# First stage of a fused forward-and-backward block re-ordered: gate row and grad_out loaded first, sines and norms of x in pinned orders, first w2^T products between the turns of grad_out

## The chip, the cores and the metric

The kernel runs on one core of a Trainium2 chip. A core has five engines, each with an instruction queue of its own that is worked in order: TensorE (PE in the profile; its weight loads are listed as PEld), VectorE (DVE), ScalarE (ACT), GpSimd (POOL) and SyncE (SP), which here only issues transfers. Engines wait for each other and for transfers through semaphores. Transfers run on 16 DMA engines that all queues share. The metric is the time of one execution on the device in microseconds (us).

## The reference

The reference computes one block and all its gradients. For x of 2048 tokens by 1024, with `c` a 1024-long condition:

```python
mod = (silu(c) @ w_mod)                      # six rows of 1024: sa, ca, ga, sb, cb, gb
h = layernorm(x) * (1 + ca) + sa
x = x + ga * irfft2(rfft2(h) * (w_r + 1j * w_i))
h = layernorm(x) * (1 + cb) + sb
x = x + gb * (gelu(layernorm(h) @ w1 + b1) @ w2 + b2)      # w1: 1024 x 3584
```

It returns x and, for a given `grad_out`, the gradients by x, w_r, w_i, w1, b1, w2, b2, c and w_mod. The Fourier transforms are computed in the kernel as matrix products with tables of sines and cosines, after the even and odd parts of h were split by additions and subtractions ("folds").

## The kernel before, in words

The program is written against a tile library. When the kernel is built, a planner gives every instruction a place in its engine's queue, and it chooses the engine where the code says `nc.any`. `tc.high_priority()` moves an instruction ahead in that plan, and `with tc.issue_after(ins)` pins what is written under it behind `ins`. Tiles that carry the same `tag` share memory, so a later tile waits for the last use of the earlier one.

The part that matters here is the first stage, up to the first spectral product (`pu`, line 472). It has four strands.

- **Rows of mod.** `mod_load` brings a 1024 x 512 block of w_mod (1 MB), `mod_block` (line 246) multiplies it with silu(c) in eight products into PSUM (`pm`, line 253), and DVE or ACT copies the result to a row (line 256). Row 5 is gb, row 1 is ca, row 0 is sa. The blocks use a ring of three buffers.
- **grad_out, turned.** `load_go` brings grad_out in four quarters of 1 MB. PE turns each in eight groups of four 128 x 128 transposes (`pt`, line 344), and DVE and ACT in turn copy a group out of PSUM, multiplied with gb per row (`gBoT`, lines 347 and 351). gb has to stand as a column for that (`gb_col`, line 339, from the little products `pc`, line 337). Four PSUM buffers of tag "f" serve these groups, and the same four serve the w2^T products below.
- **Sines.** `trig` (line 389) lets POOL make an integer index (line 373, into a ring of two index buffers), DVE mask it (line 396), and ACT take the sine (line 397). `gen_mats` does this for eight pieces of the row tables (smA, smB) and four of the column tables (em1), stores them to DRAM, and scales a copy of em1 on POOL (line 412).
- **x.** `load_tok` brings a chunk of 512 tokens, half of it by one SP transfer and half by two gathers that POOL issues (line 131). `ln_dve` or `ln_mix` computes mean and variance (BN statistics on DVE, lines 437 and 447; sums on ACT, lines 451 and 454), `ln_fin` the reciprocal root, `norm_act` (line 461) normalises on ACT in four instructions, and DVE multiplies with 1 + ca and folds (line 173). The first `pu` product needs all four chunks.

The time between is filled with the w2^T products: `ph_part` (line 678; `pp`, line 684) multiplies w2^T, loaded by a transposing transfer of 256 rows (`load_w2t`, line 301, two buffers), with gBoT. 28 row chunks of four quarters with eight products each are made in all; they are independent of x. ACT and DVE copy the results (lines 691, 694) and POOL issues their store (line 696). Further row blocks of mod are computed between them.

SP's queue before has this order: c, ca block 0, x0, ca block 1, gb block 0, grad_out 0, gb block 1, w2^T 0, grad_out 1, x1, grad_out 2 and 3, x2, x3, w2^T 1, then sa and the later blocks. POOL's has x's eight gathers ahead of all index work.

Of the kernel before, what the change touches and what calls it, by code (L numbers as in the profile page):

```python
# [11 lines left out]
BF16 = mybir.dt.bfloat16  # L12
# [23 lines left out]
def kernel(  # L36
# [88 lines left out]

    def load_tok(t4, src, i, eng=None):
# [3 lines left out]
        for q in range(2):  # L130
            nc.gpsimd.indirect_dma_start(out=t4[:, 1 + q, :], out_offset=None, in_=s3,
                                         in_offset=bass.IndirectOffsetOnAxis(ap=xidx[:, 2 * i + q:2 * i + q + 1], axis=0))
# [114 lines left out]
    def mod_block(r, h, wblk=None):  # L247
# [4 lines left out]
        for jc in range(NDC):  # L252
            nc.tensor.matmul(pm[:], lhsT=u_b[:, jc, :], rhs=wblk[:, jc, :], start=(jc == 0), stop=(jc == NDC - 1))
        dst = MOD_DST[r][:, h * KH:(h + 1) * KH]
        with tc.high_priority():
            nc.any.tensor_copy(out=dst, in_=pm[:])
        if r in (1, 4):
            nc.vector.tensor_scalar(out=dst, in0=dst, scalar1=1.0, scalar2=None, op0=ALU.add)

# [40 lines left out]
    def load_w2t(fg):  # L300
# [4 lines left out]
    gos = [reg.tile([P, 4, D], BF16, name="go0", tag="px1")[:], reg.tile([P, 4, D], BF16, name="go1", tag="smb")[:],  # L305
           fbuf[:, 2], fbuf[:, 3]]
# [28 lines left out]
    pc = ps_d("pc")  # L335
    for cch in range(NDC):
        nc.tensor.matmul(pc[:, cch:cch + 1], lhsT=gb_row[0:1, cch * P:(cch + 1) * P], rhs=ones_bf[0:1, 0:1], start=True, stop=True)
    with tc.high_priority():
        nc.vector.tensor_copy(out=gb_col[:], in_=pc[:, 0:NDC])
    for j in range(4):  # L340
        for cch in range(NDC):
            pt = psum.tile([P, BW], BF16, tag="f", name="pt", bufs=4)
            for a in range(4):
                nc.tensor.transpose(pt[:, a * P:(a + 1) * P], gos[j][:, a, cch * P:(cch + 1) * P], ident[:])
            if cch % 2 == 0:
                with tc.high_priority():
                    nc.vector.tensor_scalar(out=gBoT[j][:, cch, :], in0=pt[:], scalar1=gb_col[:, cch:cch + 1], scalar2=0.0,
                                            op0=ALU.mult, op1=ALU.add, accum_out=gu[:, j, cch:cch + 1])
            else:
                with tc.high_priority():  # L350
                    nc.scalar.activation(out=gBoT[j][:, cch, :], in_=pt[:], func=ACT.Identity, scale=gb_col[:, cch:cch + 1],
                                         accum_out=gu[:, j, cch:cch + 1])

# [17 lines left out]
    def pts(out, in0, s1, s2, o0, o1=None):  # L371
        kw = {} if o1 is None else {"op1": o1}
        nc.gpsimd.tensor_scalar(out=out, in0=in0, scalar1=s1, scalar2=s2, op0=o0, **kw)
# [15 lines left out]
    def trig(dst, colv, rowv, nrow, width, modn, cosine):  # L389
# [3 lines left out]
        for r in range(nrow):  # L393
            pts(idx[:, r * width:(r + 1) * width], colv, rowv[:, r:r + 1], sh, ALU.mult, ALU.add)
        n = nrow * width
        nc.vector.tensor_scalar(out=idx[:, 0:n], in0=idx[:, 0:n], scalar1=modn - 1, scalar2=None, op0=ALU.bitwise_and)
        nc.scalar.activation(out=dst, in_=idx[:, 0:n].rearrange("p (r w) -> p r w", w=width), func=ACT.Sin,
# [969 lines left out]
```

## Time and profile before

| | |
|---|---|
| median of 3 runs | 1463.76 us (1459.1 to 1466.73) |
| profiled execution | 1459.13 us; span of its trace 1457.3 us |
| PE busy | 1396.5 us, 96% of the span |
| DVE, ACT, POOL busy | 73%, 52%, 25% |
| gb's column copied (`gb_col`) | at 29.65 us |
| last scaled copy of grad_out | from 45.23, read out by 45.98 us |
| last fold of x (fourth chunk) | from 127.58 us |
| first spectral stage `pu` in full | 129.41 us |
| first product of the second layer (`pz`) | 343.87 us |

Times within the trace count from the start of the span. In a timeline row stand the start, the busy time, the engine and line, the operation with the tiles it writes and reads, the shape, the number of instructions merged into the row, and in brackets how long the engine had stood idle and what released it. The view by windows gives, for stretches of time, the busy time of each engine with the number of instructions, the clock that TensorE was granted (1.00 is full), the mean busy share of the DMA engines and GB/s.

### The profile page before, as it was taken

How to read it: one execution, taken by the hardware profiler on the slowest of the kernel's cores; microseconds unless marked ns; L12 is line 12 of the kernel's file. 1: busy time of each engine (PE TensorE's matmuls, PEld its weight loads, DVE VectorE, ACT ScalarE, POOL GpSimd, SP SyncE). 2: the span in 40 equal slices, each digit the busy share in tenths (PEclk: the TensorE clock that was granted, in tenths of full speed). 3: DMA queues.
4: the chain of work that ended last, by engine and by line, in shares of the span. 5: the costliest groups of instructions: out<-in, count | busy, mean ns of one | idle time of the engine just before them, and what ended most of it. 6: DMA issues, size and time to landing. Idle time of an engine off the chain costs nothing. (4 is left out here: it accounts for less than half of the span.)

```text
span 1457.3 us, 18411 instructions
## 1 busy us (share of the span) xinstructions
PE 1396.5 (96%) x6835; PEld 649.0 (45%) x6835; DVE 1058.4 (73%) x1483; ACT 752.2 (52%) x1065; POOL 366.1 (25%) x441
## 2 busy tenths in 40 slices
PE   5889999999999999999999999999999999999997
PEld 2434545444444444444444444344444445444443
DVE  5884786898799787887520889898467678898650
ACT  4675555857887766665305574342622434344211
POOL 6520451211112122122211011021245441222432
PEclk8999999999999999999999999999999999999999
DMA  9962473899887877697998275297699987766991
GB/s 333 286 214 70 142 235 115 270 255 337 257 203 278 259 250 233 201 264 241 277 297 245 74 271 185 107 270 176 181 217 254 254 233 213 194 191 180 297 279 65
DMA packets 358367, 324.28 MB, mean 223 GB/s; under 512 B 209386, under 2 KB 301056, under 8 KB 358022
## 3 DMA queue, kind: packets, MB, share of 16 engines
q1 hardware_dynamic: 324166, 207.71, 52.7%
q0 software_dynamic: 34112, 115.41, 22.6%
q8 instruction: 53, 0.87, 0.2%
q14 instruction: 36, 0.29, 0.1%
HBM read 162.06 MB, written 111.20 MB: 188 GB/s over the span
## 5 line engine op out<-in xcount | busy, mean ns | idle before, releaser
L684 PE MATMUL pp<-gBoT,wt 128*128 128x512 bf16 x896 | 197.9, 380 | 4.5 <-DMA wt<-in_B_w_dram 2.6
L950 PE MATMUL pg<-w1T,gzr 128*128 128x512 bf16 x896 | 197.1, 381 | 0.2 <-ACT gn3b L961 0.2
L1266 PE MATMUL gw1acc<-gzh,n3n 128*128 128x512 bf16 x896 | 195.4, 379 | 1.3 <-DMA gzh<-d_gz 1.3
L684 PEld LDWEIGHTS <-wt 128*128 128x128 bf16 x896 | 87.7, 98 | 109.4 <-issue 4.2
L950 PEld LDWEIGHTS <-gzr 128*128 128x128 bf16 x896 | 87.3, 98 | 108.7 <-issue 6.6
L802 PEld LDWEIGHTS <-w 128*128 128x128 bf16 x896 | 87.3, 98 | 108.8 <-issue 4.7
L1266 PEld LDWEIGHTS <-n3n 128*128 128x128 bf16 x896 | 87.4, 98 | 106.1 <-issue 2.7
L802 PE MATMUL pz<-n3Tb,w 128*128 128x512 bf16 x448 | 99.2, 379 | 1.6 <-DVE w2sD L875 1.4
L802 PE MATMUL pz<-n3Ta,w 128*128 128x512 bf16 x448 | 98.7, 379 | 1.1 <-ACT gt L805 1.1
L1075 PE MATMUL gw2acc<-gB,hhsA 128*128 128x512 bf16 x448 | 98.5, 379 | 1.0 <-DMA hhsA<-d_hh 1.0
L853 PEld LDWEIGHTS <-hhA 128*128 128x128 bf16 x608 | 59.0, 98 | 71.7 <-issue 1.4
L805 ACT ACTIVATE gt<-pz,b_col 128x512 bf16<-128x512 f32 x112 | 72.5, 684 | 34.2 <-PE pz L802 32.8
L1270 ACT CAST gwo<-gw1acc 128x512 bf16<-128x512 f32 x50 | 29.1, 583 | 113.6 <-PE gw1acc L1266 99.0
L173 DVE TENSOR_TENSOR gt<-gt,gt 128x2048 bf16<-128x2048 bf16 x56 | 68.3, 1223 | 22.4 <-ACT gt L813 21.2
L1082 ACT CAST gwo<-gw2acc 128x512 bf16<-128x512 f32 x46 | 26.7, 583 | 109.9 <-PE gw2acc L1075 75.6
L811 ACT ACTIVATE gt<-gt 128x2048 bf16<-128x2048 bf16 x28 | 53.5, 1910 | 55.7 <-DVE gt L173 55.7
L173 DVE TENSOR_TENSOR ct<-ct 128x2048 bf16<-128x2048 bf16 x64 | 75.9, 1218 | 1.8 <-DMA d_n<-ct 1.1
L1075 PEld LDWEIGHTS <-hhsA 128*128 128x128 bf16 x448 | 43.6, 98 | 53.0 <-DMA hhsA<-d_hh 1.7
L997 DVE CUSTOM_DVE_ANT_0 otl<-otl 128x1024 bf16<-128x1024 bf16 x24 | 29.1, 1223 | 49.9 <-DMA otl<-in_w_mod_dram 44.2
L807 ACT ACTIVATE gt<-gt 128x2048 bf16<-128x2048 bf16 x28 | 53.4, 1908 | 5.4 <-DVE hhC L173 2.5
L813 ACT ACTIVATE gt<-gt 128x2048 bf16<-128x2048 bf16 x28 | 53.5, 1909 | 0.5
L1271 POOL DMA_DIRECT2D out_dram<-gwo x56 | 30.6, 548 | 85.6 <-ACT gwo L1270 53.4
(325 smaller groups left out, 2531.5 us busy)
## 6 DMA issues: line engine op xcount, KB each, us to landing
gzr<-d_gz SPq DMA_DIRECT2D x28, 512.0 KB
wblk<-in_w_mod_dram SPq DMA_DIRECT2D x12, 1024.0 KB
out_dram<-otl POOLq DMA_DIRECT2D x48, 256.0 KB
out_dram<-gwo POOLq DMA_DIRECT2D x96, 128.0 KB
d_ph<-pho POOLq DMA_DIRECT2D x21, 512.0 KB
d_hh<-hhA POOLq DMA_DIRECT2D x19, 512.0 KB
w2sD<-in_B_w_dram SPq DMA_DIRECT2D x14, 512.0 KB
hhC<-d_ph SPq DMA_DIRECT2D x14, 512.0 KB
```

The source lines that it names most:

```text
L173: return nc.vector.tensor_tensor(out=out, in0=a, in1=b, op=op)
L684: last_pe[0] = nc.tensor.matmul(pp[:], lhsT=wt[:, fg % 2, cch, k * P:(k + 1) * P], rhs=gBoT[j][:, cch, :], start=(cch == 0), stop=(cch == ...
L802: last_pe[0] = nc.tensor.matmul(pz[:], lhsT=w1s[g][:, cch, k * P:(k + 1) * P], rhs=n3T[:, cch, :], start=(cch == 0), stop=(cch == NDC - 1))
L805: nc.scalar.activation(out=zb[:, k, :], in_=pz[:], func=ACT.Identity, bias=b1_col[:, fc:fc + 1], scale=1.0)
L807: nc.scalar.activation(out=av, in_=zb, func=ACT.Square)
L811: nc.scalar.activation(out=sg, in_=bv, func=ACT.Sigmoid, scale=2.0 * GK)
L813: nc.scalar.activation(out=bv, in_=bv, func=ACT.Sigmoid, scale=-2.0 * GK)
L853: last_pe[0] = nc.tensor.matmul(pbs[i][:], lhsT=hh[:, k, i * P:(i + 1) * P], rhs=wp[:, k, :], start=False, stop=(g == 6 and k == 3))
L950: last_pg[0] = nc.tensor.matmul(pgs[i][:], lhsT=gzs[b, g][:, k, i * P:(i + 1) * P], rhs=w1Ts[g][:, k, h * KH:(h + 1) * KH], start=(g == 0 ...
L1075: nc.tensor.matmul(acc[:], lhsT=hh_of(fc)[:, t, :], rhs=gBs[t // 4][:, t % 4, h * KH:(h + 1) * KH], start=(t == 0), stop=(t == NT - 1))
L1266: nc.tensor.matmul(acc[:], lhsT=n3ns[t // 4][:, t % 4, cch * P:(cch + 1) * P], rhs=gz2[t // 8][:, t % 8, :], start=(t == 0), stop=(t == NT ...
L1271: nc.gpsimd.dma_start(out=out_4[cch * P:(cch + 1) * P, fg * 512:(fg + 1) * 512], in_=ob)
```

## The change

The first stage is written in another order; no operation of the computation is added or removed.

- SP's queue now has: c, gb block 0, gb block 1, x0, grad_out 0 to 3, w2^T 0, ca block 0, ca block 1, x1, x2, x3, w2^T 1, sa block 0, sa block 1, then the later blocks. grad_out 0 takes the memory of tag "ot", grad_out 1 to 3 lie in `fbuf`.
- The row tables are made first: four pieces (index, mask, sine) stand ahead of x0's gathers on POOL, two more ahead of x1's, two more ahead of those of x2 and x3. The copy of gb's second half is pinned to DVE behind the fourth mask. The column tables, their scaling and all stores of tables come behind the norms of x1.
- ACT's order is pinned: the first four sines, its copies of grad_out 0, then the square root and the four norms of x0, then its copies of grad_out 1, 2 and 3, then the other sines.
- PE's order is pinned from the first turn on: grad_out 0, 1 and 2, the 16 products of w2^T chunks 0 and 1 with quarter 0, grad_out 3, ca's two blocks, then chunks 0 and 1 with quarters 1 to 3. sa's blocks follow within chunk 2.
- The norms of x1 to x3 are pinned behind the fold of the chunk before.

```diff
@@ loads @@
-    mod_get(1, 0)
-    load_tok(x4s[0], A_x, 0)
-    mod_get(1, 1)
     mod_get(5, 0)
-    for h in range(2):
-        mod_block(1, h, wm[1, h][:])
     mod_get(5, 1)
-    load_go(0)
-    load_w2t(0)
-    load_go(1)
-    load_tok(x4s[1], A_x, 1)
-    load_go(2)
-    load_go(3)
-    for h in range(2):
-        mod_block(5, h, wm[5, h][:])
-    load_tok(x4s[2], A_x, 2)
-    load_tok(x4s[3], A_x, 3)
-    load_w2t(1)
...
+    rows_of = gen_rows()
+    for _ in range(4):
+        next(rows_of)
+    with tc.issue_after(gen_in["pool"].ins):
+        load_tok(x4s[0], A_x, 0)
+    for j in range(4):
+        load_go(j)
+    load_w2t(0)
+    mod_block(5, 0, wm[5, 0][:])
+    with tc.issue_after(gen_in["dve"].ins):
+        mod_block(5, 1, wm[5, 1][:], nc.vector.tensor_copy)
+    for h in range(2):
+        mod_get(1, h)
...
+    def go_turned(j):
+        for cch in range(NDC):
+            pt = psum.tile([P, BW], BF16, tag="f", name="pt", bufs=4)
+            for a in range(4):
+                with ordered() if last_pe[0] is not None else ExitStack():
+                    last_pe[0] = nc.tensor.transpose(pt[:, a * P:(a + 1) * P], gos[j][:, a, cch * P:(cch + 1) * P], ident[:])
+            if cch % 2 == 0:
+                with tc.high_priority():
+                    dve = nc.vector.tensor_scalar(out=gBoT[j][:, cch, :], in0=pt[:], scalar1=gb_col[:, cch:cch + 1], scalar2=0.0,
+                                                  op0=ALU.mult, op1=ALU.add, accum_out=gu[:, j, cch:cch + 1])
+            else:
+                with tc.high_priority(), tc.issue_after(act_in.ins):
+                    act = nc.scalar.activation(out=gBoT[j][:, cch, :], in_=pt[:], func=ACT.Identity, scale=gb_col[:, cch:cch + 1],
+                                               accum_out=gu[:, j, cch:cch + 1])
+        return act, dve
+
+    act_in, _ = go_turned(0)
+    with tc.issue_after(act_in.ins), tc.issue_after(gbc_in.ins):
+        ln_dve(x4s[0], 0, 0)
+        act_in = norm_act(fbuf[:, 0], x4s[0], 0, 0)
+    for j in range(1, 4):
+        act_in, go_dve = go_turned(j)
+        if j == 2:
+            for fc in range(2):
+                ph_part(fc, (0,))
+    act_go = act_in
+    with tc.issue_after(act_in.ins):
+        for _ in range(2):
+            next(rows_of)
+        with tc.issue_after(gen_in["pool"].ins):
+            load_tok(x4s[1], A_x, 1)
+        for _ in rows_of:
+            pass
+        with tc.issue_after(gen_in["pool"].ins):
+            for i in (2, 3):
+                load_tok(x4s[i], A_x, i)
+        x_gathers = g_in[0]
+    with ordered():
+        for h in range(2):
+            last_pe[0] = mod_block(1, h, wm[1, h][:])
+    for j in range(1, 4):
+        for fc in range(2):
+            ph_part(fc, (j,))
+    load_w2t(1)
+    for h in range(2):
+        mod_get(0, h)
...
     for fc in range(PH_EARLY):
-        ph_part(fc, (0, 1, 2, 3))
+        if fc > 1:
+            ph_part(fc, (0, 1, 2, 3))
+        if fc == 1:
+            with ordered():
+                for h in range(2):
+                    last_pe[0] = mod_block(0, h, wm[0, h][:])
...
+    folds = [go_dve]
     for i in range(4):
         x4, fb = x4s[i], fbuf[:, i]
-        if i == 0:
-            with tc.issue_after(u_in.ins):
-                ln_dve(x4, 0, i)
-        elif i > 0:
-            ln_mix(x4, 0, i, fb)
...
-        norm_act(fb, x4, 0, i)
+        if i > 0:
+            with tc.issue_after(act_go.ins), tc.issue_after(folds[i - 1].ins):
+                ln_mix(x4, 0, i, fb)
+                act_go = norm_act(fb, x4, 0, i)
+        if i == 1:
+            with tc.issue_after(act_go.ins), tc.issue_after(x_gathers.ins):
+                gen_cols()
+                d_E_in = gen_store()
```

More of the change, by code (lines that the diff above doesn't have):

```diff
@@ L304 @@
     fbuf = reg.tile([P, 4, 4, D], BF16, name="fbuf", tag="fr")
-    gos = [reg.tile([P, 4, D], BF16, name="go0", tag="px1")[:], reg.tile([P, 4, D], BF16, name="go1", tag="smb")[:],
-           fbuf[:, 2], fbuf[:, 3]]
+    gos = [reg.tile([P, 4, D], BF16, name="go0", tag="ot")[:]] + [fbuf[:, j] for j in range(1, 4)]
     def load_go(j):
@@ L460, in norm_act @@
             t = 4 * i + q
-            nc.scalar.activation(out=out4[:, q, :], in_=in4[:, q, :], func=ACT.Identity,
-                                 scale=stats[:, row, 0, t:t + 1], bias=stats[:, row, 1, t:t + 1])
+            ins = nc.scalar.activation(out=out4[:, q, :], in_=in4[:, q, :], func=ACT.Identity,
+                                       scale=stats[:, row, 0, t:t + 1], bias=stats[:, row, 1, t:t + 1])
+        return ins
+    rows_of = gen_rows()
+    for _ in range(4):
+        next(rows_of)
@@ new lines @@
+    with tc.issue_after(gen_in["pool"].ins):
[8 more added lines that the diff above has]
+        mod_get(1, h)
+    pc = ps_d("pc")
+    for cch in range(NDC):
+        nc.tensor.matmul(pc[:, cch:cch + 1], lhsT=gb_row[0:1, cch * P:(cch + 1) * P], rhs=ones_bf[0:1, 0:1], start=True, stop=True)
```

127 lines of the change are left out of this document (60 added, 67 removed).

## The prediction, made before the changed kernel ran

> **What bounds the kernel now.** First I read the page: TensorE (PE) is busy 96% of the span, so time can only go where PE stands idle or runs at half clock. The page's chain of what ended last is no help here (it adds up to under a tenth of the span), so I went by stretches: the busy time in 10 us windows, then PE's timeline, then who waited for whom.
>
> ```profile
> PE 1396.5 (96%) x6835; PEld 649.0 (45%) x6835; DVE 1058.4 (73%) x1483; ACT 752.2 (52%) x1065; POOL 366.1 (25%) x441
> ...
> 10.00:20.00 10.00, 5.20 (x13) 1.62 (x13) 7.08 (x18) 1.66 (x3) 8.56 (x13) 0.90 1.05 379
> 20.00:30.00 10.00, 5.16 (x37) 2.34 (x35) 2.50 (x9) 8.04 (x9) 3.18 (x5) 0.84 1.07 337
> 30.00:40.00 10.00, 6.92 (x72) 6.05 (x73) 9.93 (x26) 8.13 (x21) 3.88 (x6) 0.75 0.99 359
> ```
>
> The window columns are PE, weight loads, VectorE (DVE), ScalarE (ACT), GpSimd (POOL), granted clock, DMA share, GB/s. PE is half idle, the DMA share is 1: the first 40 us are set by loads. PE's timeline has the three places that matter:
>
> ```profile
> 29.36 0.26 PE L337 MATMUL pc<-ones_bf,rows 1*128 1x1 bf16 x4 [3.21 <-DVE rows L256]
> ...
> 45.36 5.12 PE L684 MATMUL pp<-gBoT,wt 128*128 128x512 bf16 x23 [0.43 <-DVE gBoT L347]
> ...
> 128.32 0.60 PE L472 MATMUL pu<-smA,fbuf 128*128 128x512 bf16 x2 [0.60 <-DVE fbuf L173]
> ...
> 330.05 13.99 PE L684 MATMUL pp<-gBoT,wt 128*128 128x512 bf16 x64 [2.62 <-DMA wt<-in_B_w_dram]
> ```
>
> So gb's column, without which no turned grad_out leaves PSUM, is ready only at 29.8; the turns end at 45.4; and at 128.3 the first spectral product waits for DVE's last fold of x. From 45.98 (the last of the scaled copies) to that fold, in five stretches, this was the sum:
>
> ```profile
> sum 82.32, PE 74.02 PEld 32.40 DVE 70.29 ACT 52.20 POOL 27.79; mean PE 14.80 PEld 6.48 DVE 14.06 ACT 10.44 POOL 5.56
> ```
>
> DVE is busy 70.3 of 82.3 there: this is DVE's stretch, PE fills it with w2^T products, and the two arrive within 0.6 us of each other. Two rows of DVE for later, one slow, one waiting:
>
> ```profile
> 62.52 4.67 DVE L173 TENSOR_TENSOR x<-fbuf 128x2048 bf16<-128x2048 bf16 x1
> ...
> 115.67 2.29 DVE L173 TENSOR_TENSOR fbuf<-fbuf,rows 128x4096 bf16<-128x4096 bf16 x1 [0.38 <-ACT fbuf L461]
> ```
>
> **The change, step by step.** All times below follow the changed program's order on each queue.
>
> *1. Loads.* Nothing is added or dropped; SP's order becomes gb's two blocks, x0, four grad_out quarters, w2^T 0, then ca's blocks and the other x. Before, SP's queue had moved 0.86 MB by 5 us and with POOL's 1.90 MB in the next five: 0.38 MB/us. With 1.05 MB a block, gb's second block lands at 5+(2.10-0.86)/0.38 = 8.3 (it was multiplied at 24.25 before), grad_out 0 at 12.4, grad_out 3 at about 22. What falls behind them, ca, x1 to x3 and w2^T 1, lands by 45 and is first read at 42.8 (ca), 43 (x1) and 57: covered. SP's later waits are on PE steps that are done 15 us and more before the use. Without that cover (ca late) PE would wait as in 51.89, 1.4 us.
>
> *2. Sines ahead on POOL, DVE, ACT.* POOL now makes four index pairs (1.5 to 2 us each) before it issues x0's two gathers: the fourth needs ACT's second sine, so the gathers are issued at 13.2 and 14.4 instead of 4.74 and 6.09. Before, the first gather's reader was released 6.9 us after its issue; the same gives 20 and 21.5. gb's second half is copied by DVE behind the fourth index mask, at 13.8; the column stands at 15.2. Gain at this point: 29.8-15.2 = 14.6.
>
> *3. The pin that gives it back.* ACT does grad_out 0's scaled copies, then x0's square root and four norms, and only then grad_out 1's copies. The root needs DVE. DVE from 15.2: eight scaled copies at 0.67 (5.4), eight BN statistics at 0.62 (5.0), four aggregates and one mask (1.0): 26.6. Root 0.3, reciprocal and product 0.4, four norms at 1.16 (4.6): 32.0. Four scaled copies of grad_out 1 at 0.67: 34.7. PSUM has four buffers for turns; ACT's four hold them all, so PE stands from 21 to 32.7. Grad_out 2's turns and copies go to 36.5 on PE, and the 16 products of w2^T now set between the turns follow. They cost 16 x 0.216 = 3.5 at full clock and 6.9 at half. After such pauses the clock is half: 0.50 between 28 and 34 before, 1.00 only from 35. I take 5.0, since one such low stretch (3.4 us long at 18.0) covers about half of them. Grad_out 3's turns wait for the products' copies; the last scaled copy ends 3 us later, at 44.6 (43.1 to 46.5 by the two clocks). Before: 45.98. So of 14.6 us only 1.4 are left.
>
> The Trainium skill, TensorE: Matmul & The Clock Gate, "Part 1", says that one idle window of some 3.4 us halves the clock and one busy window restores it. By that rule one half-rate window falls on these products, 1.7 us more than full clock, 5.2 in all. The rows (0.50 for two windows on end, at 28 to 35) would allow the full 3.4 more.
>
> *4. DVE's stretch to the spectral stage.* Past the turns DVE has more left than before: seven BN statistics (x1, x2 were begun early before) 4.3, three aggregates 0.3, one more evacuation 0.6, two row additions 0.5: 5.7. So 70.3+5.7 = 76.0 busy. Idle was 12.0. In the new order I find three waits, each for ACT's norms (4.6 us) of x1, x2, x3, less what DVE has in between: 1.0, 1.2 and 3.4: 5.6. Bounds: 3.4 (only x3's) and 12 (as before). 44.6+76.0+5.6 = 126.2 against 128.3: 2.1 us earlier; by the bounds 4.3 earlier to 4.3 later. Beside the row of 4.67 (1.21 is the usual) POOL runs its 5.60 us scaling and then a memset, which cost DVE some 4.7 us; in the new order they fall on x1's folds instead of x0's, so the same 4.7 stays in the 76.0. ACT gets three more table loads (1.28 each): 3.8 us, at 44, 61 and 83, where DVE is the later one; they also delay one copy that PE needs at 78.6, 1.6 us, which the wait at the gate swallows.
>
> The Trainium skill, SBUF — State Buffer, "Who interferes with whom", calls the port shared by DVE and GpSimd an exclusive lock, the loser blocked for the whole instruction, but only against GpSimd reads. By it the scaling alone could cost its whole 5.60 and the memset nothing: 5.6 for 4.7, a gate 0.9 later. The trace has a 2.40 us DVE row beside the memset, which speaks against the second half.
>
> *5. Sixteen products banked.* Up to the gate PE does 16 more w2^T products than before. PE reaches it at 44.6 + (82.3 - 10.4 of idle and half clock) + 3.5 + some 3.5 of new waits = 123.5, so they fit under DVE. The spectral stage keeps its fillers; they are missing from the run of w2^T products at 256 to 330, which gets 3.5 us shorter. That run ends in the 2.62 us wait of the row at 330.05. There SP's load stood behind a store of d_n3 that waits for DVE (issued 314.42); in the new order it stands ahead of that store. So I count the 3.5 as kept; lower bound 0, if the load lands no earlier.
>
> *Sum:* -2.1-3.5 = -5.6 us. Everything after is the same program with PE at 97%. The profiled execution took 1459.1 (span 1457.3, 1.8 around it), so 1453.5 in its like; the median of the three runs, 1463.8, is 4.6 above it: 1458.2.
>
> **The rivals.**
> *A: back at the gate.* The gain of step 5 is lost in the wait for w2^T, or DVE idles 9 us instead of 5.6. For: DVE was within 0.6 us of PE, and the DMA share is 1.06 in 320 to 340. Gain 0 to 2.1: 1463.8 to 1461.7.
> *B: more.* DVE meets POOL's scaling with statistics instead of folds and its only wait is x3's: 2.2 and up to 4.7 less. PE then sets the gate at 123.5: -4.8-3.5-1 for a shorter wait at 330: 1454.5. Against: ACT is full from 72 to 92.
> *C: slower, x0's gathers.* They now start while 4 MB of grad_out are queued. Every us that the second lands after 23.0 (DVE's turn for it) moves norms, turns and everything behind. At 28.6 the gain is gone; from 36 on the kernel is over 0.5% slower. If they share poorly and land when SP's 11.5 MB are through (39), it is 16 us: 1474. For: POOL's queue got 0.14 MB between 5 and 10 us. Against: 1.11 MB in the next five, a share above SP's.
>
> **How the numbers follow.** About 0.5% (7.3 us) is what a measurement here can tell from no change. Chances: forecast 0.43, A 0.24, B 0.18, C with lesser stalls of its kind 0.15. Predicted: 1458.2. Range: from B less 3 us (the runs spread 0.25% about their median) to halfway to C: 1451 to 1469. Faster by 0.5%: B and a tenth of the forecast's spread, 0.23. Slower: most of C and a little of A, 0.15. Same: 0.62.
>
> **What the profile after would show.** Step 1 and 2: the pc products at about 15, grad_out turns from 13. Step 3: PE idle some 11 us up to 33, released by ACT's copy, and ACT's four norms just before. Step 4: pu's third product released by DVE's fold at about 126, PE idle 1 to 3 us there. Step 5: eleven products fewer before the first pz, the pz at about 338. I am wrong if the gathers land after 23, if the turns end after 47, or if DVE's stretch is much off 82 us.

## The result and the profile after

The changed kernel takes 1469.85 us (median of 22 runs, 1465.75 to 1478.25), the kernel before 1464.17 us (22 runs, 1458.38 to 1471.04). The ratio is 1.0041, with a 95% interval of 1.0028 to 1.0053: some 6 us slower. The forecast was 1458.2 us, 5.6 us faster, with a range up to 1469.

The profiled execution of the changed kernel took 1478.25 us (span 1476.5), the slowest of its runs; that of the kernel before, 1459.13 us, was one of its fastest. Their difference of 19 us is therefore not the effect of the change, and the traces are compared stretch by stretch. The first line of the page after:

```profile
PE 1402.1 (95%) x6835; PEld 652.0 (44%) x6835; DVE 1061.5 (72%) x1484; ACT 755.2 (51%) x1067; POOL 387.5 (26%) x441
```

The view by windows of the first 40 us (PE, PEld, DVE, ACT, POOL, clock, DMA share, GB/s):

```profile
10.00:20.00 10.00, 7.08 (x64) 4.67 (x63) 7.51 (x19) 7.58 (x12) 8.53 (x11) 0.92 1.05 397
20.00:30.00 10.00, 2.34 (x16) 1.69 (x16) 7.56 (x23) 2.60 (x5) 1.92 (x2) 0.50 1.11 347
30.00:40.00 10.00, 6.68 (x42) 4.50 (x42) 3.03 (x8) 7.97 (x20) 0.00 (x0) 0.56 1.11 298
```

PE's work has moved forward into 10 to 20 us, and 20 to 30 us are nearly empty. PE's timeline after shows what happened at the places that the prediction spoke of:

```profile
15.06 0.25 PE L457 MATMUL pc<-ones_bf,rows 1*128 1x1 bf16 x4 [0.85 <-DVE rows L258]
...
33.05 1.25 PE L495 MATMUL pt<-ident,fbuf 128*128 128x128 bf16 x8 [9.49 <-ACT gBoT L502]
...
37.15 4.45 PE L474 MATMUL pp<-gBoT,wt 128*128 128x512 bf16 x16
...
130.54 0.60 PE L545 MATMUL pu<-smA,fbuf 128*128 128x512 bf16 x2 [0.79 <-DVE fbuf L175]
...
330.66 5.34 PE L474 MATMUL pp<-gBoT,wt 128*128 128x512 bf16 x24 [1.83 <-DVE phr L481]
...
374.34 12.25 PE L854 MATMUL pz<-n3Ta,w 128*128 128x512 bf16 x56 [1.73 <-ACT gt L857]
...
387.09 1.89 PE L854 MATMUL pz<-n3Ta,w 128*128 128x512 bf16 x8 [0.50 <-ACT gt L857]
...
406.13 7.07 PE L854 MATMUL pz<-n3Ta,w 128*128 128x512 bf16 x32 [2.90 <-ACT gt L857]
```

gb's column is ready 14.3 us earlier (copied at 15.35 instead of 29.65), and DVE's last scaled copy of grad_out is still read out at 44.64 against 45.98 (ACT's at 45.22 against 45.97). `pu`'s products on the earlier chunks of x run from 109.38 us (before from 111.30); the `pu` row that needs the fourth chunk, the gate in what follows, comes 2.2 us later than before (130.54 against 128.32) instead of 2.1 earlier. Behind it PE waits for ACT at three `pz` rows. In the trace of before there is one such wait over 0.2 us:

```profile
400.84 7.07 PE L802 MATMUL pz<-n3Ta,w 128*128 128x512 bf16 x32 [1.12 <-ACT gt L805]
```

To follow a delay through the program, I use one figure, worked out from the traces: of the instructions of DVE that two traces have in common, the median by which they start later than in the first trace of before. I call it DVE's lag. For the changed kernel it is +4.8 us at 200 to 240 us, +6.9 at 320 to 360 and +4.7 from 440 to 700 us.

### Where the 4.8 us at 200 us come from

**DVE's stretch from the turns to the gate.** By windows, from 44.64 to 130.5:

```profile
sum 85.86, PE 77.36 PEld 34.12 DVE 76.83 ACT 55.37 POOL 45.51; mean PE 15.47 PEld 6.82 DVE 15.37 ACT 11.07 POOL 9.10
```

DVE is busy 76.8 us (forecast 76.0) and idle 9.0 (forecast 5.6). Nearly all the idle time has rows in DVE's timeline after:

```profile
53.54 0.69 DVE L365 TENSOR_SCALAR gidx<-gidx 128x1024 int32<-128x1024 int32 x1 [0.70 <-POOL gidx L340]
...
63.02 0.43 DVE L365 TENSOR_SCALAR gidx<-gidx 128x512 int32<-128x512 int32 x1
...
66.83 0.43 DVE L365 TENSOR_SCALAR gidx<-gidx 128x512 int32<-128x512 int32 x1 [0.28 <-POOL gidx L340]
...
73.66 2.29 DVE L175 TENSOR_TENSOR fbuf<-fbuf,rows 128x4096 bf16<-128x4096 bf16 x1 [0.89 <-ACT fbuf L438]
...
76.90 0.43 DVE L365 TENSOR_SCALAR gidx<-gidx 128x512 int32<-128x512 int32 x1 [0.35 <-POOL gidx L340]
...
79.33 0.43 DVE L365 TENSOR_SCALAR gidx<-gidx 128x512 int32<-128x512 int32 x1 [0.86 <-POOL gidx L340]
...
80.92 5.69 DVE L175 TENSOR_TENSOR fbuf<-x 128x2048 bf16<-128x2048 bf16 x2
...
98.37 2.29 DVE L175 TENSOR_TENSOR fbuf<-fbuf,rows 128x4096 bf16<-128x4096 bf16 x1 [1.34 <-ACT fbuf L438]
...
114.90 0.69 DVE L484 CAST pho<-pp 128x512 bf16<-128x512 f32 x1 [2.43 <-PE pp L474]
...
116.62 0.69 DVE L481 CAST pho<-pp 128x512 bf16<-128x512 f32 x1 [1.03 <-PE pp L474]
...
117.89 2.29 DVE L175 TENSOR_TENSOR fbuf<-fbuf,rows 128x4096 bf16<-128x4096 bf16 x1 [0.57 <-ACT fbuf L438]
```

The waits for the norms of x1 (0.89), x2 (1.34) and x3 (2.43 + 1.03 + 0.57; in the first two DVE stood before copies that wait for PE, while the norms were not done either) are 6.3 us, close to the forecast 5.6. The four waits for an index table from POOL (0.70, 0.28, 0.35, 0.86: 2.2 us) I had not booked at all.

**The gathers of w.** In the spectral stage POOL issues gathers of w's mirrored rows. POOL's and DVE's timelines, first before:

```profile
170.28 4.75 POOL L491 DMA_INDIRECT ws<-in_A_w_r_dram,xu  x1 [3.64 <-DVE qa L173]
...
175.91 6.22 POOL L491 DMA_INDIRECT ws<-in_A_w_i_dram,xu  x1 [0.30 <-issue]
...
183.02 2.06 POOL L491 DMA_INDIRECT ws<-in_A_w_r_dram,xu  x1 [0.30 <-issue]
...
185.68 1.23 DVE L173 TENSOR_TENSOR qb<-Pt,ws 128x2052 bf16<-128x2052 bf16 x1 [1.45 <-DMA ws<-in_A_w_i_dram,xu]
```

and then after, with PE's wait that follows:

```profile
172.38 4.78 POOL L564 DMA_INDIRECT ws<-in_A_w_r_dram,xu  x1 [3.09 <-DVE qa L175]
...
177.46 6.79 POOL L564 DMA_INDIRECT ws<-in_A_w_i_dram,xu  x1 [0.30 <-issue]
...
185.72 6.28 POOL L564 DMA_INDIRECT ws<-in_A_w_r_dram,xu  x1 [0.30 <-issue]
...
193.95 1.23 DVE L175 TENSOR_TENSOR qa<-Pt,ws 128x2052 bf16<-128x2052 bf16 x1 [2.85 <-issue]
...
200.00 8.38 PE L638 MATMUL pv<-smi,R 128*128 128x512 bf16 x32 [2.84 <-DVE V L720]
```

Before, DVE happened to stand 1.45 us at 184, and the third gather was issued in 2.06 us beside that pause. After, DVE did not pause there; the third gather took 6.28 us beside an unbroken run of DVE's products, and DVE then stood 2.85 us before the product that reads its rows (the view names no releaser for this wait). From the first `pcs` product to the first `po` product the traces show 50.8 us before and 53.4 after: 2.6 us lost, which with 2.2 at the gate makes the 4.8. The third gather shown here sorts all traces that have gathers, but for e5's, whose order is another one: where it took 2.05 or 2.06 us (before, e1, e9, e10, e12 and e13 below) the stretch is 48.1 to 51.0 us long, where it took 6.27 to 6.32 (after, e2, e3, e4, e11 and e14) 53.4 to 56.2.

### The profile page after: what moved, and what is told of

Its sections match the earlier page's. It is cut to its first block, busy times and chain, and to the rows that moved or that the text cites. A ratio compares the mean times of both kernels' runs of the same rounds, so it can differ in the third digit from the quotient of the medians.

```text
span 1476.5 us, 18411 instructions
## 1 busy us (share of the span) xinstructions
PE 1402.1 (95%) x6835; PEld 652.0 (44%) x6835; DVE 1061.5 (72%) x1484; ACT 755.2 (51%) x1067; POOL 387.5 (26%) x441
## 5 line engine op out<-in xcount | busy, mean ns | idle before, releaser
L859 ACT ACTIVATE gt<-gt 128x2048 bf16<-128x2048 bf16 x28 | 53.4, 1908 | 5.3 <-DVE hhC L175 2.4
L865 ACT ACTIVATE gt<-gt 128x2048 bf16<-128x2048 bf16 x28 | 53.4, 1909 | 0.5
L1323 POOL DMA_DIRECT2D out_dram<-gwo x56 | 30.8, 552 | 82.2 <-ACT gwo L1322 48.1
```

The costliest lines, as they stand in the source:

```text
L859: nc.scalar.activation(out=av, in_=zb, func=ACT.Square)
L865: nc.scalar.activation(out=bv, in_=bv, func=ACT.Sigmoid, scale=-2.0 * GK)
L1323: nc.gpsimd.dma_start(out=out_4[cch * P:(cch + 1) * P, fg * 512:(fg + 1) * 512], in_=ob)
```

## The experiments

Columns: start of the `pu` row that DVE's last fold releases ("gate"), DVE's lag at 200 to 240 us and at 480 to 520 us, and the ratio of the median to that of before in the same comparison. Every experiment changes the kernel after, except e8, e9, e13 and e15, which start from the kernel before.

| run | gate | lag at 200 | lag at 480 | time, ratio [95%] |
|---|---|---|---|---|
| before | 128.32 | 0 | 0 | |
| after | 130.54 | +4.8 | +4.7 | 1469.85, 1.0041 [1.0028, 1.0053] |
| e1 products behind the turns | 133.18 | +3.8 | +3.6 | 1467.58, 1.0028 [1.0002, 1.0054] |
| e2 sixteen products left out | 130.69 | +5.0 | +7.1 | 1468.86, 1.0040 [1.0013, 1.0067] |
| e3 scaling on ACT | 127.25 | +3.3 | +5.6 | 1471.50, 1.0051 [1.0030, 1.0071] |
| e4 norms of x0 behind the copies | 125.47 | -0.2 | +5.2 | 1473.65, 1.0066 [1.0045, 1.0087] |
| e5 e4 with the old shares of copies | 129.09 | +3.9 | +17.2 | 1483.97, 1.0124 [1.0091, 1.0157] |
| e6 rows of w direct | 129.04 | -0.9 | -1.0 | 1472.88, 1.0035 [1.0011, 1.0059] |
| e7 e5 and e6 | 127.95 | -2.3 | +11.6 | 1480.30, 1.0097 [1.0064, 1.0130] |
| e8 before, rows of w direct | 126.67 | -3.2 | -3.6 | 1468.87, 1.0002 [0.9978, 1.0027] |
| e9 before, scaling on ACT | 127.19 | -2.4 | -2.7 | 1465.19, 1.0002 [0.9982, 1.0021] |
| e10 statistics of x1 early | 133.22 | +2.2 | +4.5 | 1475.43, 1.0072 [1.0045, 1.0099] |
| e11 e10 and e3 | 132.10 | +9.2 | +11.9 | 1479.02, 1.0096 [1.0082, 1.0111] |
| e12 e1, e10 and e3 | 129.62 | +1.2 | +5.6 | 1471.61, 1.0041 [1.0017, 1.0065] |
| e13 before, again | 125.99 | -2.1 | -1.4 | one trace |
| e14 after, again | 130.73 | +5.2 | +5.2 | one trace |
| e15 e8, again | 126.99 | -2.9 | -2.8 | one trace |

The theory at the start: the changed kernel loses at the gate, and what is lost or won there carries to the end. The rivals: PE's own amount of work sets the time (P), or the loss comes from behind the gate. e2 leaves out half of the sum over channels in one row chunk, and e6, e7, e8 and e15 bring w's mirrored rows in ascending order: their results are not the reference's, and they serve for timing alone.

### e1: the 16 products behind the turns

```diff
         act_in, go_dve = go_turned(j)
-        if j == 2:
-            for fc in range(2):
-                ph_part(fc, (0,))
...
-    for j in range(1, 4):
+    for j in range(4):
         for fc in range(2):
             ph_part(fc, (j,))
```

> The changed kernel with one part undone: the 16 products of w2^T that stood between grad_out 2's and grad_out 3's turns come behind all the turns. Theory V (VectorE's lag): from the turns to 400 us the end follows VectorE, which was 2.2 us late at the gate (x3's last fold) and 4.8 late from 200 us on, and PE's lead of products is waited away between 360 and 420 us. Then the last scaled copy comes at 40 instead of 44.6, VectorE begins its stretch 4.5 us earlier, the gate is at 126 to 127 instead of 130.5, and the kernel is 3.5 to 4.5 us faster than the changed one: 1465.4 to 1466.4, ratio to the kernel before 1.001 to 1.0015. Rival P (PE's own time): the products have to be done somewhere, PE is the bound, and the time stays within 1 us of 1469.9, ratio 1.004.

PE's turns ended 3.9 us earlier (40.3 instead of 44.2), and yet the gate was 2.6 us later. DVE began its stretch earlier and idled 13.1 us in it, against 9.0: the time that it gained came back as waits. DVE's timeline of this run has, among others:

```profile
56.00 0.76 DVE L365 TENSOR_SCALAR gidx<-gidx 128x512 int32<-128x512 int32 x1 [2.99 <-POOL gidx L340]
...
67.99 0.69 DVE L258 CAST sar<-pm 128x512 bf16<-128x512 f32 x1 [1.10 <-PE pm L255]
```

The first wait is not that of a late producer: POOL had this table, the first of the column tables, done at 55.96, and in after only at 62.98. But the planner put its mask (56.00 here, 63.02 without any wait in after) ahead of the folds that follow it here; they read only what DVE itself had made by 52.93, and stood behind the mask in DVE's queue. At 480 us this kernel is nevertheless 1.1 us ahead of the changed one, because its gathers fell better (49.7 us from `pcs` to `po`).

### e2: sixteen products of the second layer's w2^T left out

```diff
-            for cch in range(NDC):
+            last = 3 if fc == 20 else NDC - 1
+            for cch in range(last + 1):
```

> The changed kernel without 16 of the 32 products of block 20 of w2^T times grad_out (the second half of the sum over channels), which PE does at about 300 us. It leaves 3.5 us of PE's work out, at the place where the prediction booked the 16 early products as a gain. Theory V: PE waits these 3.5 us away before 420 us because ScalarE and VectorE set the pace there; the time is that of the changed kernel within 1 us, 1469 to 1471, ratio 1.0035 to 1.0045. Rival P: PE is the bound and the kernel is 3.5 us faster than the changed one, 1466.4, ratio 1.0015.

3.5 us of PE's work were taken out of the run of w2^T products, and the median did not fall: 1.0040 against 1.0041. The interval of 1.0013 to 1.0067 still holds the 1.0015 that rival P expects, so the times alone do not decide. The trace speaks against P: the lag at 480 us is 7.1, larger than in after. PE's timeline of this run shows where the 3.5 us went:

```profile
315.85 29.34 PE L475 MATMUL pp<-gBoT,wt 128*128 128x512 bf16 x128 [4.08 <-DMA wt<-in_B_w_dram]
...
392.60 7.07 PE L855 MATMUL pz<-n3Ta,w 128*128 128x512 bf16 x32 [2.08 <-ACT gt L858]
...
408.09 8.58 PE L855 MATMUL pz<-n3Ta,w 128*128 128x512 bf16 x32 [4.97 <-ACT gt L858]
```

PE waits 4.1 us for w2^T, so that its first `pz` comes no earlier than in after (345.03 against 344.83), and then 7.1 for ACT, against 5.1 in after. What PE has less to do is paid back as waiting. The edit is not quite alone, though: behind 330 us the order of DVE's and ACT's instructions differs from that of after, and what that does to the 7.1 is not separated.

### e3: the scaling of the column tables on ACT

```diff
-        nc.gpsimd.tensor_scalar(out=em1[:, 1], in0=em1[:, 0], scalar1=2.0 / (S * D), scalar2=None, op0=ALU.mult)
+        nc.scalar.activation(out=em1[:, 1], in_=em1[:, 0], func=ACT.Identity, scale=2.0 / (S * D))
```

> The changed kernel with one instruction on another engine: the scaling of the em matrices (128x2048, 5.53 us on GpSimd at 80.6, beside which a VectorE pair of folds took 5.69 us instead of 2.36) is done by ScalarE. Theory V: the pair takes 2.4 us, the gate comes 3.3 to 4.4 us earlier (126 to 127), and so does the end: 1465.5 to 1466.6, ratio 1.001 to 1.002. Rival P: PE reaches the gate at 129.7 in any case, so the gain is at most 0.8 us: 1469, ratio 1.0035 to 1.004.

The gate came 3.3 us earlier, as expected, and DVE's two folds beside the scaling, 5.69 us at 80.92 in after, took

```profile
80.15 2.36 DVE L175 TENSOR_TENSOR fbuf<-x 128x2048 bf16<-128x2048 bf16 x2
```

So the 3.3 us are POOL's doing. Nothing of it reached the end. DVE's lag had shrunk by 1.5 at 200 us (the gathers held it up 1.8 us longer than in the changed kernel) and was 0.9 larger at 480.

### e4: x0's root and norms behind all copies of grad_out

```diff
-    with tc.issue_after(act_in.ins), tc.issue_after(gbc_in.ins):
-        ln_dve(x4s[0], 0, 0)
-        act_in = norm_act(fbuf[:, 0], x4s[0], 0, 0)
+    with tc.issue_after(gbc_in.ins):
+        ln_st = ln_dve(x4s[0], 0, 0, False)
     for j in range(1, 4):
...
+    with tc.issue_after(act_in.ins):
+        ln_fin(*ln_st)
+        act_in = norm_act(fbuf[:, 0], x4s[0], 0, 0)
```

> The changed kernel with one pin moved: ScalarE does the square root and the four norms of x0 behind all scaled copies of grad_out, instead of between grad_out 0's and grad_out 1's. Theory V: PE's idle 9.5 us up to 33.05 goes, the turns end at 35 to 38 instead of 44.6, VectorE's hole of 6 us at 27.6 closes, and the gate comes 3 to 7 us earlier (123 to 127); the end moves as much, 1463 to 1467, ratio 0.999 to 1.002. Rival L (the loads and x1 to x3 bind): the statistics of x1 to x3 wait for their gathers, the gate stays at 129 to 131 and the time within 1 us of 1469.9.

PE's turns ended at 34.9 instead of 44.2 and the gate came 5.1 us earlier, the best gate of all variants. The kernel was no faster than the changed one (1.0066 against 1.0041, the intervals overlap). So an earlier gate does not carry to the end; my first theory had to go. DVE's lag of -0.2 at 200 us grew to +5.8 at 360. Where, shows ACT's timeline: the root of the second norm (first row) and a GELU step (second), in before,

```profile
376.21 0.30 ACT L427 ACTIVATE mv<-mv,eps_c 128x4 f32<-128x4 f32 x1
...
396.50 1.91 ACT L811 ACTIVATE gt<-gt 128x2048 bf16<-128x2048 bf16 x1 [3.63 <-DVE gt L173]
```

in after,

```profile
381.66 0.30 ACT L404 ACTIVATE mv<-mv,eps_c 128x4 f32<-128x4 f32 x1 [1.23 <-DVE mv L415]
...
401.79 1.91 ACT L863 ACTIVATE gt<-gt 128x2048 bf16<-128x2048 bf16 x1 [3.63 <-DVE gt L175]
```

and in e4:

```profile
382.76 0.30 ACT L404 ACTIVATE mv<-mv,eps_c 128x4 f32<-128x4 f32 x1 [3.01 <-DVE mv L415]
...
401.68 1.91 ACT L868 ACTIVATE gt<-gt 128x2048 bf16<-128x2048 bf16 x1 [3.62 <-DVE gt L175]
```

In e4 the root stands behind a wait of 3.01 us for DVE's statistics and is no earlier than in after, although everything at 200 us was 5 us earlier. This stretch, in which DVE and ACT hand statistics and GELU steps to each other, comes out of the planner in another order in most variants that start from after (more under "What stays open").

### e5 and e7: the old shares of copies behind the gate

A rival explained e4 by the copies that the planner gives to DVE or ACT: they differ between before and after. e5 is e4 with each copy behind the gate on the engine that it had in before, written out as a list; e7 adds e6's edit.

```diff
+    def any_copy(out, in_):
+        if plan_at[0] is None:
+            return nc.any.tensor_copy(out=out, in_=in_)
+        e = PLAN[plan_at[0]]
+        plan_at[0] += 1
+        return (nc.vector.tensor_copy if e == "D" else nc.scalar.copy)(out=out, in_=in_)
...
-                    nc.any.tensor_copy(out=ov, in_=pv)
+                    any_copy(out=ov, in_=pv)
```

> The kernel with x0's norms behind the turns (which had its gate 2.9 us ahead of the kernel before, its first projection po level with it, and was 5.6 us late at 480 us), with one thing more: every copy out of PSUM behind the gate that the planner may give to VectorE or ScalarE is given to the engine that it had in the kernel before. Theory G (gathers and plan): behind the gate there were two losses, one at GpSimd's gathers of w (165 to 205 us), one in VectorE's full stretch from 230 to 400 us, where the planner had given VectorE 13 of the 24 later copies of po instead of 7. With the old shares the second goes: the lag at 480 us is that of the first po, about 0, and the time 1463.5 to 1465.5, ratio to the kernel before 0.9995 to 1.001. Rival Q (the pace is set by something else than the shares): the lag at 480 stays at 5 to 6 us and the time at 1472 to 1474.

> Both at once: x0's norms behind the turns, the old shares of the copies behind the gate, and plain transfers in place of GpSimd's gathers in the forward spectral stage (the mirrored rows of w in the wrong order). Theory G: nothing is left that gives the earlier gate back, and its 2.9 us and 1 to 1.5 us of the gathers arrive at the end: 1460 to 1461.5, ratio 0.997 to 0.998. Rival Q: another wait takes their place behind 230 us, and the time is 1464 or more.

Both became much worse (+17.2 and +11.6 us at 480). The list fixes the engine and not the order. So the old shares alone do not bring e4's loss back; why they make it worse is not shown.

### e6 and e8: the rows of w by plain transfers

Only the forward pass's gathers go, in after (e6) and in before (e8). `w_minus` is a plain transfer on SP's queue of the same number of rows, in ascending order.

```diff
-                nc.gpsimd.indirect_dma_start(out=ws[:, x, 1, 0:DF], out_offset=None, in_=w, in_offset=w_idx(par, m))
+                if fwd:
+                    w_minus(ws[:, x, 1, 0:DF], w, par, m)
+                else:
+                    nc.gpsimd.indirect_dma_start(out=ws[:, x, 1, 0:DF], out_offset=None, in_=w, in_offset=w_idx(par, m))
```

> The changed kernel without GpSimd's 16 gathers of w's mirrored rows in the forward spectral stage: the same number of rows comes by plain transfers from the sync queue, in ascending order, so the mirrored half of the products of w is computed from rows in the wrong order; the other engines' order is that of the changed kernel. Theory G: VectorE's unbroken stream holds a gather up to 6.8 us (rows of 4.78, 6.79 and 6.28 at 172 to 192 us), VectorE then waits 2.85 us for the rows and PE 2.84 us for VectorE; without the gathers the time from the first pcs to the first po falls from 53.4 to 49 to 50 us, the lag of 4.8 us at 210 becomes 0.5 to 1.7, and the kernel takes 1465.5 to 1467, ratio 1.001 to 1.002. Rival Q: VectorE's own work sets this stage, the first po stays at 210 to 211 us and the time at 1469 to 1471.

> The kernel before, with plain transfers in place of GpSimd's 16 gathers of w in the forward spectral stage (the mirrored rows in the wrong order). Theory G: there the held gathers (4.75 and 6.22 us) cost VectorE one wait of 1.45 us and PE one of 1.21 us; 1 to 1.5 us faster, 1463 to 1463.4, ratio 0.999. If the gathers cost the kernel before as much as the changed one, it is 2.6 us or more faster: then they are no part of the difference.

Both kernels now take 49.1 to 49.2 us from `pcs` to `po`. Against that the gathers cost before 1.6 us and after 4.2, which confirms the 2.6 us between them. (It is no floor: e10 and e12, with gathers, took 48.1 and 48.4.) In e6 the waits of DVE and PE are gone there; PE's timeline at that place:

```profile
189.23 0.59 PE L645 MATMUL pv<-smi,R 128*128 128x512 bf16 x2
189.66 0.60 PE L585 MATMUL pcs<-em,U 128*128 128x256 bf16 x4
190.32 12.33 PE L645 MATMUL pv<-smi,R 128*128 128x512 bf16 x56
```

But the ends did not follow: e6, with a lag of -1.0 up to 780 us, measured 1.0035, and e8, 3.6 us ahead, 1.0002. The two ran in one comparison and are 4.0 us apart, against 5.7 with the gathers in both; the intervals are too wide to say whether the 2.6 us reach the end. In their traces the lead goes behind 700 us, for the most part in waits of PE for transfers (11.5 and 11.8 us there, 3.6 in the first trace of before).

e6 shows one thing more. Behind 205 us DVE's and ACT's instructions stand in the order of after, DVE is 0.9 us ahead of before instead of 4.8 late, and PE still waits 5.1 us for ACT at three `pz` rows, as in after. The longest:

```profile
400.10 7.07 PE L861 MATMUL pz<-n3Ta,w 128*128 128x512 bf16 x32 [2.89 <-ACT gt L864]
```

So these waits follow PE's lead over the chain of ACT and DVE, and not the lateness of that chain.

### e9: before with the scaling on ACT

The edit is e3's, in the kernel before.

> The kernel before with one instruction on another engine: ScalarE instead of GpSimd scales the em matrices (beside GpSimd's scaling a VectorE row took 4.67 us instead of 1.21). Theory L (lag and lead): the end follows VectorE's lag when the first projection po comes, which is the shift of the gate plus what the gathers of w cost between the first pcs and the first po (49.2 us without a held gather, 50.8 in the kernel before, 53 to 55 where two are held); PE's lead of w2^T products is worth nothing, and above some 280 at the gate it costs. Gate 3.5 us earlier (124.1), then 1.6 us less to 4.3 us more at the gathers: between 1459.5 and 1465, most likely 1461, ratio 0.998. Rival Q (the gate carries nothing to the end): within 1 us of the kernel before whatever the gate does, ratio 1.000.

The gate was 1.1 us earlier, DVE 2.7 us ahead at 480, and its profiled execution took 1457.16 us. Against the second trace of before (e13, below) the gate is 1.2 us later and the lead at 480 only 1.3. Its median is that of before (1.0002). With e8 it is the nearest to a gain of all variants, and none that can be measured.

### e10, e11 and e12: work moved into DVE's hole at 37 us

DVE stands idle in the changed kernel from 37.7 to 41.9 us. e10 puts the statistics of x1 there; e11 adds e3, e12 adds e1 and e3.

```diff
+            go2_dve = go_dve
...
+        with tc.issue_after(go2_dve.ins):
+            x1_mv = mix_stats(x4s[1])
...
-                ln_mix(x4, 0, i, fb)
+                ln_mix(x4, 0, i, fb, x1_mv if i == 1 else None)
```

> The changed kernel with one pin loosened: VectorE's share of x1's statistics (four of 0.67 us, two aggregates and one scale, 3.1 us) stands in its hole before grad_out 3's scaled copies (idle 4.14 us at 37.7) instead of behind them. Theory L: VectorE's stretch to the gate has 3.1 us less to do and the gate comes at 126 to 127.5 instead of 129.8; with the changed kernel's 4.2 us at the gathers the end is 2 to 3 us earlier, 1467 to 1468, ratio 1.002 to 1.0025; with no held gather it is 5 to 7 us earlier, ratio 0.9995. Rival W (waits): the work was not what held the gate, ScalarE's norms and GpSimd's index tables were; VectorE idles longer instead, gate 129 to 130, ratio 1.004.

> The changed kernel with x1's statistics in VectorE's hole and the em scaling on ScalarE. Theory L: gate at 123 to 124.5; with PE's lead at 285 to 295 products the gain is given back between 330 and 420 us as in the runs with a lead of 285 and 291 (2.3 and 5.8 us): lag at 480 us between 0 and 5 us, ratio 1.000 to 1.0045. If the lead costs nothing, the lag is -6 to 0 and the ratio 0.996 to 1.000.

> The changed kernel with three things: the 16 products behind the turns, x1's statistics ahead of them as they fit, the em scaling on ScalarE. Theory L: the run with the 16 products behind had its gate at 132.4 and a lead of 267; 3.1 and 3.4 us less put the gate at 126 and the lead stays below 280, so nothing is given back between 330 and 420 us: lag at 480 us -3 to +3 by the gathers, ratio 0.998 to 1.002. Rival Q: as the other variants, 5 us behind the kernel before, ratio 1.0035.

Less work was left for the stretch, and the gate came 2.7 us later. DVE's timeline of e10:

```profile
59.25 0.76 DVE L365 TENSOR_SCALAR gidx<-gidx 128x512 int32<-128x512 int32 x1 [3.01 <-POOL gidx L340]
...
69.82 0.43 DVE L756 TENSOR_SCALAR sar<-sar 128x1024 bf16<-128x1024 bf16 x1 [1.61 <-ACT sar L258]
...
102.93 2.29 DVE L175 TENSOR_TENSOR fbuf<-fbuf,rows 128x4096 bf16<-128x4096 bf16 x1 [2.52 <-ACT fbuf L442]
```

From 44.64 to the gate DVE was busy 2.4 us less than in after and idle 5.1 us more (14.2 against 9.0). The largest wait is that of e1 again: the mask of the first column table stands ahead of the next folds, and waits 3.01 us for a table that cost nothing in after (63.02). x2's norms cost 2.52 instead of 1.34. DVE's stretch is not "work plus a few waits": what POOL and ACT have ready, and where the planner sets DVE's instructions that need it, bound it too, within 2 or 3 us each. e11 fell worst into the gathers (56.2 us from `pcs` to `po`) and e12, whose gate is the best of the three, lost 4.4 us between 200 and 480: neither beat the kernel before.

### e13, e14 and e15: before, after and e8 once more

The lag at 480 us did not match the end in every case, so I took a second trace of three kernels, unchanged.

> The kernel before once more, unchanged. Theory L: what is lost or not lost between 700 us and the end is a matter of the single execution (its waits for transfers), so this trace agrees with the first trace of before within 0.5 us up to 480 us and differs from it by some 3 to 12 us at the end, with waits of PE for transfers at 738 or behind 1000. Rival M: the late waits belong to the changed programs; then this trace stays within 1 us of the first all the way.

> The changed kernel once more, unchanged. Theory L: a lag of 4.7 us behind the first trace of before at 480 to 700 us, as in its first trace, within 0.5; behind that another figure than the 10.7 at 780 and 19 at 1300. Rival M: again 10.7 at 780 and 19 at 1300, within 1.

> The kernel before with plain transfers in place of the forward gathers of w once more (rows of w in ascending order, so another result). Theory L: 3.6 us ahead of the first trace of before at 480 to 700, and a loss behind that which differs from the first trace's (+0.3 at 780, +14 at 1300). Rival M: the same losses at the same places, within 1: the lead is eaten by a transfer that comes at a fixed time.

Behind 700 us the executions of one program differ. DVE's lag of after was 10.7 at 780 us in the first trace and 5.1 in the second; the waits of PE for transfers, behind 700 us, in the first trace (total, count, longest),

```profile
PE pbo L905 <- DMA w2sC<-in_B_w_dram: 4.2, 1, 4.2
...
PE gw2acc L1127 <- DMA hhsA<-d_hh: 3.3, 2, 2.6
...
PE gw2acc L1127 <- DMA otl<-d_hh: 1.7, 1, 1.7
```

and in the second:

```profile
PE gw2acc L1127 <- DMA hhsA<-d_hh: 4.4, 2, 3.0
PE gw2acc L1127 <- DMA otl<-d_hh: 3.1, 2, 2.7
```

In all they are 9.5 and 8.6 us, at other places; the two traces of before have 3.6 and 5.2. The second trace of before lost 10.2 us between 480 us and the end against its first, behind 700 us for the most part, where PE waited 9.3 us longer: 4.0 for ACT, 3.5 for DVE and 1.6 for transfers. So the 14.4 of the 19 us between the first two profiles that after lost behind 480 us need not be the change's: in the second traces before lost 10.2 us there and after 8.8.

What I had not expected is that the first 480 us of before vary too: its gate was 2.3 us earlier in the second trace, 125.99. 1.4 us of that is a wait of DVE for a block of mod, 2.21 us in the first trace and 0.85 in the second. So the expected agreement within 0.5 us up to 480 failed for before, and held for after, which repeated within 0.2 us at the gate and 0.5 at 480. Of two traces each, the mean difference at 480 us is (4.7 + 5.2)/2 - (0 - 1.4)/2 = 5.6 us, and the medians differ by 5.7. That agrees with a slowdown that is made before 480 us, but two traces of each do not prove it. e5, e7 and e11, the latest at 480, are the slowest in time too. In e6, e8 and e9 the lag at 480 was 2.7 to 5.7 us less than in the kernel they start from, and no gain could be measured at the end; in no experiment did a lag that was taken away show measurably in the time.

For e8 the second trace repeated the lead (2.8) and the loss behind it (14 us, 18 in the first). That is more than in either trace of before; whether the plain transfers cause it is not shown.

## Why the prediction was wrong

**Steps 1 and 2, loads and sines: right.** The `pc` products ran at 15.06 and the column was copied at 15.35 (forecast 15.2). x0's gathers were issued at 13.96 and 15.65 (forecast 13.2 and 14.4) and held nobody up; rival C did not come.

**Step 3, the pin that gives it back: right, and close in each number.** Root at 26.79 (26.6), norms done at 32.3 (32.0), PE idle until 33.05 (32.7) for 9.5 us (some 11), 16 products in 4.45 us (5.0), DVE's last scaled copy read out at 44.64 (44.6) and ACT's at 45.22. In windows of 2 us the granted clock was 0.50 up to 38 us, 0.79 from 38 to 40 and 1.00 behind: the 4.45 us stand between full clock (3.5) and half (6.9), and the full 3.4 us more did not come. The Trainium skill, TensorE: Matmul & The Clock Gate, "Part 1", with one window at half rate gave an estimate of 5.2; the trace is nearer to that than to the 6.9.

**Step 4, DVE's stretch: the sum was missing terms.** Forecast 126.2, measured 130.54: 4.3 later than forecast, 2.2 later than before, and inside the bounds of the text (124.0 to 132.6, from 3.4 to 12 us of idle time). In place of 5.6 us of idle time there were 9.0: 2.2 us of waits for POOL's index tables, which the step did not name although the trace of before had one (0.86 at 59.28), and 0.7 more for the norms. Busy time was 0.8 over. The scaling was right in kind and too dear: 3.3 us on the 5.69 row, not its whole 5.53, and nothing beside the memset (1.22 and 2.36 us rows there), where the step had 4.7 for both. This is rival A's "DVE idles 9 us instead of 5.6", to the figure. A was priced too mildly: with 9 us of idle time the step's own sum puts the gate at 129.6, 1.3 us later than before, and A stayed a gain only because it took either this or the loss of step 5, "or", and not both. Both came, the second by waits for ACT.

**Step 5, sixteen products banked: the work was saved and the time was not.** PE came to its first `pz` with a lag of 1.0 us (344.83; forecast 338), although it had started `po` 4.8 late: the 3.5 us were there, and the wait at 330 was 0.8 shorter. Then PE waited 5.1 us for ACT at three `pz` rows, against 1.1 before, and its lag at 480 us was 4.7. The second traces show the same: 1.73, 0.50 and 2.90 us again in after, no wait over 0.2 in before. The step looked only at the wait for w2^T as what could swallow the gain, because PE was busy 97%. It should have asked who releases PE next: ACT, with its chain through DVE, over which PE's lead had grown. e6 has these waits too, without DVE's lateness. e2, with as much of PE's work left out, shows both waits: for w2^T (4.1) and for ACT (7.1).

**"Everything after is the same program": wrong in two ways.** The gathers of w cost 2.6 us more, with the same instructions, because DVE's run met them in another phase: the traces show it at the third gather, and e6 and e8 without gathers take equally long. And the planner places copies and norms behind the gate anew when something ahead of it changes (e4). Neither was a rival.

The terms as measured: +2.2 (gate) + 2.6 (gathers) + 0 (banked) = +4.8 us, in place of -2.1 - 3.5 = -5.6. These are lags within the traces, up to 480 us; that they are what the median of the time lost is likely by their size and not shown by an experiment. The reference of 128.32 was itself one execution: between the second traces the gate lost 4.7 us, the gathers 2.6 again, and the lag at 480 us is 6.6.

**What stays open.** Why variants that reach 200 us earlier lose 2 to 6 us by 480 (e3, e4, e10, e12), and e5 and e7 over 13. It is not the gate, nor simply how many w2^T products PE has issued by the gate (counted in the traces): e10 (270), e11 (279) and e12 (258) lost 2.3 to 4.4 us, while after with 277 and e1 with 267 lost nothing. One thing in the traces sorts the runs: the share of ACT's 247 instructions of 205 to 480 us that stand in the order of before (the longest sequence that both traces have in common). It is 0.83 to 1.00 in all that lost under 1 us between 200 and 480 (after, e1, e6, e8, e9 and the second traces) and 0.71 to 0.81 in all that lost 2 to 14 (e2, e3, e4, e5, e7, e10, e11, e12). That points at the planner's order; no run here changes the order alone, so the cause is not shown. Open too is why e6, e8 and e9 show nothing of their lead at the end.

## What to carry to other kernels

An engine that is busy nine tenths of a stretch is still bounded by its producers: before work is moved into or out of it, list every wait with every producer (here POOL's tables), and where in its queue the instructions that need them will stand, because a stretch that is started earlier can give the gain back as waiting. Work banked on an engine that later waits for another engine can be worth nothing, however busy it looks: follow the gain to the next point where someone else releases it. Where a planner orders the rest and engines disturb each other, "the same program behind" is an assumption with a price of several us, and one trace of before is not enough to compare with.

## What the runs showed of the hardware

- Of the 16 gathers of w in the forward stage two before and three after took 4.75 to 6.79 us to issue on POOL, beside unbroken runs of DVE's bf16 additions and products in SBUF; the others took 0.95 to 3.15 us. Such a run does not hold every gather (1.75 us at 164.59 in after, beside DVE's additions and products too). The long ones ended 0.9 to 1.0 us after a copy from PSUM or a pause of DVE had begun (before: copy at 181.20, end at 182.13; after: last of the run ends at 191.10, issue ends at 192.00).
- POOL's scaling of a 128 x 2048 tile took 5.53 us and stretched two folds of DVE from 2.36 to 5.69 us: the first took 4.55 us, the second its usual 1.21, and began at 85.40 while the scaling still ran (to 86.13). With the same scaling on ACT the two took 2.36 us, which brought the gate 3.3 us forward.
- Two executions of the kernel before ended 8.8 us apart: the second was 2.3 us ahead at the gate and lost 10.2 us behind 480 us, where PE waited longer for ACT, DVE and transfers.
